# Attention with global rows and a two-layer MLP on one core: a transposition of gathered rows moved by one pair, three casts spread out, masks built earlier

## The chip, the cores and the metric

The kernel runs on one core of one Trainium2 chip. The metric is the device time of one execution in microseconds (us). A kernel is executed several times, and the times given are medians with the lowest and highest. All executions here counted as fast ones but one, the 368.65 us of e9_wst, which lies over 1.5% above that kernel's fastest; ratios leave it out. Each comparison was made on one chip, with the kernel before executed in the same rounds. A profile is one traced execution; its span is a little shorter than the time of that execution (368.7 us against 370.33 for the kernel before). Numbers of single instructions come from such profiles.

## The reference

```python
# q, k, v: (8, 8, 576, 64) float32; global_idx: 8 sorted positions
mask = np.abs(pos[:, None] - pos[None, :]) <= 32
mask = mask | is_global[:, None] | is_global[None, :]
scores = np.where(mask, 0.125 * q @ k^T, -1e9)
attn = softmax(scores) @ v                      # (8, 8, 576, 64)
x = attn.transpose(0, 2, 1, 3).reshape(4608, 512)
h = x @ w_in                                    # (512, 2048)
g = s * maximum(h, 0)**2 + b
return g @ w_out                                # (2048, 512) -> float32 (4608, 512)
```

The axes are batch, head, sequence and head dimension. Each query sees a band of 65 keys and the 8 global keys; the 8 global queries see everything.

## The kernel before

The kernel treats two heads at once. There are 32 such pairs, four to a batch. Pairs 0 to 4 make up the start, where little but attention can run. From pair 5 on, each pair has eight slots, and a quantum of MLP matmuls of earlier tokens fills each slot. TensorE always has work of the MLP as long as nothing in front of it in its own list waits. The profiles show what happens when something does: while VectorE stood 7.64 us at one copy, nothing behind that copy in VectorE's list ran.

The rows of the eight global positions need extra work. They are collected by an indirect DMA (`gather`) for eight pairs at once, rounded to bfloat16 by VectorE (`round_kq`), turned by TensorE (`turn`), and put among the keys and queries of each pair (`put_kq`).

```python
def gather(bb, ts="kq"):
    ...
    for t in ts:
        nc.gpsimd.indirect_dma_start(out=gfs[bb][:, i], in_=src[t]..., in_offset=...grow[bb]...)

def globals_of(bb):
    ...
    def round_kq():                                    # L384
        nc.vector.tensor_copy(out=gb[:, 0:2], in_=gfs[bb][:, 0:2])
    def turn():                                        # L391
        for i in range(2):
            for hh in range(2):
                nc.tensor.transpose(ps[r, i], gb[r, i], ident[r, r])
    ...
    return round_kq, turn

def put_kq(p):                                         # L431: K, L435: Q
    nc.vector.tensor_copy(out=view(ktile[p], ...), in_=view(gkt[bb]...))
    nc.vector.tensor_copy(out=view(qbufs[p % 3]...), in_=view(gqd[bb % 2]...))
```

K from pair 8 on comes in its natural order (`load_nat`), is rounded by ScalarE (L189) and transposed by a DMA (`turn_k`, L224). V arrives as float32 and is cast to bfloat16 (`cast_v`, L232). The masks are small VectorE products (`build_masks`). ScalarE makes the exponentials of the scores (`e`, L510), VectorE multiplies them by the mask (`em`, L513, "the em product"), and TensorE multiplies `em` by V (`po`, L532, "P·V").

The start, and the loads that follow it:

```python
first_pair(0, {
    1: [lambda: cast_v(A, 0), lambda: build_masks((2,))],
    3: [lambda: build_masks((3, 4))],
    4: [clear_q2, lambda: select(1)],
})
flush()
steps0[0]()
load_v(nc.gpsimd, 4)
load_kq(5)
for p in (1, 2, 3):
    cast_v(G, p)                  # G: GpSimd
for p in (1, 2, 3, 4):
    first_pair(p, ...)            # with put_v, load_v(5), load_w_out(0), load_kq(6)
flush()
warm(12)                          # dummy matmuls that keep TensorE busy, L741
scatter(0)                        # GpSimd puts the global rows of batch 0 into xt, L580
load_w_out(1)
load_v(nc.gpsimd, 6)
...
load_w_out(2); load_kq(7); load_v(nc.gpsimd, 7); load_w_out(3)
```

And the loop from pair 4 on, of which the change moves two lines:

```python
for p in range(4, NPAIR):
    ...
    if p == 5:
        nc.vector.memset(natk[0:1, 0, 0, 0, 0:8], 0.0)   # holds back the load of K(8)
    for j in {4: (), 5: (8, 9), 6: (10,), 7: (11, 12)}.get(p, (p + 5,)):
        load_nat(nc.sync, "k", j); load_q(j); load_nat(nc.sync, "v", j)
    if p % 8 == 4 and p + 4 < NPAIR:
        gather((p + 4) // 8)
    ...
    if p >= 6 and p + 2 < NPAIR:
        ...                                  # round_k and round_q of later pairs, ScalarE
        at(7, turn_k, p + 2)
        at(7, put_v, None, p + 2)
    if p % 8 > 4 and p + 3 < NPAIR:
        if p % 8 == 5:
            steps = globals_of((p + 4) // 8)
            at(7, steps[0])                  # round_kq
        elif p % 8 == 6:
            at(1, steps[1])                  # turn
    if 9 <= p < 17:
        adds.extend(wpiece(p - 9))           # 0.5 MB weight pieces for the bias
```

`at(s, f)` puts `f` into slot `s` of the pair.

The softmax here doesn't subtract the row's maximum and nothing guards it: scores larger than these inputs give would overflow.

Of the kernel before, what the change touches and what calls it, by code (L numbers as in the profile page):

```python
# [54 lines left out]
def view(ap, *dims):  # L55

    return bass.AP(
        tensor=ap.tensor, offset=ap.offset, ap=[list(ap.ap[0])] + [list(d) for d in dims]
    )
# [8 lines left out]
def kernel(  # L68
# [86 lines left out]
    def load_kq(p):  # L155
        bi, hp = divmod(p, 4)
        for t in "kq":
            nc.gpsimd.dma_start(
                out=six[t][:NP6, p % NR].rearrange("p h j d -> p h (j d)"),
                in_=src[t][bi, 2 * hp : 2 * hp + 2].rearrange("h (p j) d -> p h (j d)", j=NJ),  # L160
            )

    def load_nat(eng, t, p):
        bi, hp = divmod(p, 4)
        if t == "q":
            dst = natq[:].rearrange("p n h j d -> p n (h j d)")[:, :, 0 : NCH * 2 * D]
            dst = dst.rearrange("p n (c h d) -> p n c h d", c=NCH, h=2)
        else:
            dst = natv if t == "v" else natk
        r = NG if t == "v" else 0  # L170
        for hh in range(2):
            o = src[t][bi, 2 * hp + hh, 0, 0].offset

            runs = [(0, NCH, KC)]
            if p == NPAIR - 1 and hh == 1:
                runs = [(0, NCH - 1, KC), (NCH - 1, 1, S - KC * (NCH - 1))]
            for c, nch, n in runs:
                eng.dma_start(  # L178
                    out=dst[r : r + n, p % NV, c : c + nch, hh],
                    in_=bass.AP(  # L180
                        tensor=src[t].tensor, offset=o + c * KC * D,
                        ap=[[D, n], [KC * D, nch], [1, D]],
                    ),
                )
# [9 lines left out]
    def load_q(p):  # L194
        if p >= NSIXQ:
            load_nat(nc.sync, "q", p)
            return
        bi, hp = divmod(p, 4)
        nc.sync.dma_start(
            out=natq[:NP6, p % NV].rearrange("p h j d -> p h (j d)"),  # L200
            in_=q[bi, 2 * hp : 2 * hp + 2].rearrange("h (p j) d -> p h (j d)", j=NJ),
        )
# [25 lines left out]
    def load_v(eng, p):  # L228
        load_nat(eng, "v", p)

    def cast_v(eng, p):
        eng(out=vring[:, p % NV], in_=natv[:, p % NV])  # L232
# [68 lines left out]
    def gather(bb, ts="kq"):  # L301

        if bb not in gfs:
            gfs[bb] = globp.tile([P, 3, D], FP32, tag="gf", name="gf")
        for t in ts:
            i = "kqv".index(t)
            nc.gpsimd.indirect_dma_start(  # L307
                out=gfs[bb][:, i], out_offset=None,
                in_=src[t].rearrange("b h s d -> (b h s) d"),
                in_offset=IndirectOffsetOnAxis(ap=grow[bb][:], axis=0),  # L310
            )
# [37 lines left out]
    def build_masks(cs):  # L349
        for c in cs:  # L350
            m = const.tile([P, W[c]], BF16, name=f"mask{c}", tag=f"mask{c}")
            x0 = LO[c] - P * c + WIN
            nc.vector.scalar_tensor_tensor(
                out=m[:], in0=band[:, x0 : x0 + W[c]], scalar=notg[:, c : c + 1],
                in1=gadd[c // (NCH - 1)][:, x0 : x0 + W[c]], op0=OP.mult, op1=OP.add,
            )
            masks.append(view(m[:], [0, 2], [1, W[c]]))
# [13 lines left out]
    def flush():  # L371
        ops, later[:] = list(later), []
        for f in ops:
            f()
# [297 lines left out]
    A, V, G = nc.scalar.copy, nc.vector.tensor_copy, nc.gpsimd.tensor_copy  # L672
# [40 lines left out]
    def select(p):  # L713

        ps = ps_m.tile([P, 2, NG], FP32, tag="moe", name="psg")
        for i, t in enumerate("kq"):
            for j in range(NJ):
                for hh in range(2):
                    nc.tensor.matmul(
                        ps[D * hh : D * hh + D, i], six[t][:NP6, p, hh, j], sel6[:NP6, j],  # L720
                        start=(j == 0), stop=(j == NJ - 1), skip_group_check=True,
                    )

        def put():
            nc.vector.tensor_copy(
                out=view(ktile[p], [P, NCH], [1, NG]), in_=view(ps[:, 0], [0, NCH], [1, NG])
            )
            for hh in range(2):
                r = slice(D * hh, D * hh + D)
                nc.vector.tensor_copy(  # L730
                    out=view(qbufs[p][r, hh, HB:], [P, NCH], [1, NG]),
                    in_=view(ps[r, 1], [0, NCH], [1, NG]),
                )

        later.insert(0, put)
# [7 lines left out]
    def first_pair(p, extra={}):  # L743


        if p % 4 == 0:
            open_batch(p // 4)
        bank = idle_bank()
        for s in range(NCH):
            prev, later[:] = list(later), []  # L750
            now = []
            if s > 1 if p == 0 else p > 1 or s == 0:
                warm(1, bank)
            qk(p, s)
            i = s - {0: 2, 1: 1, 4: 3}.get(p, 0)
            if i in (0, 1):
                (trans_b, trans_a)[i](p + 1, now)
            if p and s in (1, {1: 4, 4: 2}.get(p, 3)):

                pv(p - 1, (int(s == 1),))  # L760
                if s == 1:
                    pending.extend(norm_steps(p - 1))
            if s == 3 and p < 4:
                step()
            for f in prev + now:
                f()
            for f in extra.get(s, ()):
                f()
            if s == 1:
                step()  # L770
                if p == 4:
                    step()
            if s == 4 and p == 4:
                cast_v(A, 4)
# [53 lines left out]
    def clear_q2():  # L828
# [1 line left out]
        clear(qbufs[2][D:P, 0], LQ)  # L830

    first_pair(0, {
        1: [lambda: cast_v(A, 0), lambda: build_masks((2,))],
        3: [lambda: build_masks((3, 4))],
        4: [clear_q2, lambda: select(1)],
    })
    flush()
    steps0[0]()
    load_v(nc.gpsimd, 4)
    load_kq(5)  # L840
    for p in (1, 2, 3):
        cast_v(G, p)
    for p in (1, 2, 3, 4):
        first_pair(p, {
            0: [steps0[1], steps0[2]],
# [58 lines left out]
    for p in range(4, NPAIR):  # L904
        bi, hp = divmod(p, 4)
        nq = [1] * 8
        if bi == 1:
            nq = [0, 1, 1, 1, 1, 1, 1, 1] if hp else [0, 0, 0, 0, 0, 0, 1, 2]
        elif hp == 0:
            quanta[0] += 32  # L910
        if p == 5:

            nc.vector.memset(natk[0:1, 0, 0, 0, 0:8], 0.0)
        for j in {4: (), 5: (8, 9), 6: (10,), 7: (11, 12)}.get(p, (p + 5,)):
            if j < NPAIR:
                load_nat(nc.sync, "k", j)
                load_q(j)
                load_nat(nc.sync, "v", j)
# [3 lines that stand above are left out]
            for i in range(NG):  # L922
                nc.gpsimd.dma_start(
                    out=gvall[i : i + 1].rearrange("o (b h d) -> o b h d", b=B - 2, h=H),
                    in_=v[2:, :, ds(greg_p[i], 1), :].rearrange("b h o d -> o b h d"),
                )
        ex = {}

        def at(s, f, *a):
            ex.setdefault(s, []).append(lambda: f(*a))  # L930

        if p >= 6 and p + 2 < NPAIR:

            todo = {6: (8,), 8: (11,), 9: (12,)}.get(
                p, {0: (p + 3, p + 4), 3: (p + 2, p + 3)}.get(hp, ())
            )
            for i, j in enumerate(todo):
                if j < NPAIR:
                    x = 4 if p in (8, 9) else 4 * i
                    at(1 + x, round_k, j)  # L940
                    at(3 + x, round_q, j)
            at(7, turn_k, p + 2)
            at(7, put_v, None, p + 2)
        if p % 8 > 4 and p + 3 < NPAIR:
            if p % 8 == 5:
                steps = globals_of((p + 4) // 8)
                at(7, steps[0])
            elif p % 8 == 6:
                at(1, steps[1])
        if 10 <= p < 18:  # L950
            for s in (4, 7):
                if adds:
                    at(s, adds.pop(0))
        if 9 <= p < 17:
            adds.extend(wpiece(p - 9))
        if p == 18:
            assert not adds
            at(2, bias)
        if p > 18 and hp in (0, 3) and held_rows:
            at(2, release)  # L960
            at(6, release)
        run_pair(p, nq, ex)
# [43 lines left out]
```

## Time and profile before

| | kernel before |
|---|---|
| time, median of 3 (lowest to highest) | 369.65 us (367.6 to 370.06) |
| span of the profile | 368.7 us |
| TensorE busy | 346.2 us, 94% |
| longest stand of TensorE | 7.33 us at 56.4 us, for the turning of gathered rows |
| second longest | 2.52 us at 21.6 us, for V of pair 0 |
| pair 5 starts / pair 6 starts / pair 7 starts | 45.69 / 54.88 / 73.69 us |

"Pair n starts" means in this document that the first score matmul of the pair starts. The difference of two starts is how long a pair took, so the starts say where a gain arises and whether it lasts. The prediction below shows the views themselves: TensorE's row of slices first, then its waits by what ended them, then the instructions around the two longest, with the start and duration of each and, in brackets, the idle time of its engine just before and what ended it. The number after an L is a source line.

How the loads' landings were read matters as well. The instruction that issues a DMA can end long before the data arrive (the second gather's ended at 53.01 us, its rows landed at 63.45); the arrival is in the completion records of the trace. The natural K of pair 8 landed at 51.2 and 55.0 us (two halves), the two gathers of the second group at 63.02 and 63.45 us, 12.3 and 11.4 us after their issues began; the quickest gather of this kernel took 2.4 us.

The trace also records the clock that TensorE was granted. In the kernel before it changes between 1.00 and 0.50 ("full" and "half" here), among other times, at 17.04, 30.69, 58.00 and 68.24 us, in the changed kernel at 25.6, 39.25 and 42.66 us. In each kernel these times are whole multiples of 3.41 us apart; a "window" of the clock is one such stretch of 3.41 us.

Three more lines of the timeline of the kernel before are needed for the comparison, the end of the head and the rounding of the natural K of pair 8 by ScalarE:

```profile
40.40 2.76 PE L741 MATMUL psw<-dummy 128*128 128x512 bf16 x11
43.10 2.75 PE L603 MATMUL psh<-xt,win_t 128*128 128x512 bf16 x12
...
57.43 0.73 ACT L189 CAST natb<-natk 120x640 bf16<-120x640 f32 x1
```

The dummy matmuls take 2.76 us at full clock (granted 1.00 from 40.40 to 43.10 us; twelve were issued, the trace holds records of eleven), the first MLP matmuls follow at 43.10 us, and ScalarE finds its K there: no line has a bracket, so none of them waited.

### The profile page before, as it was taken

The numbers are of one execution on the slowest core, as the hardware profiler recorded it, in microseconds if no ns is written. First come the engines' busy times: TensorE is split into PE (matmuls) and PEld (weight loads), VectorE is DVE, ScalarE is ACT, GpSimd is POOL, SyncE is SP. The second block draws the span as 40 slices with busy tenths as digits, with TensorE's granted clock in tenths as the row PEclk, the third lists the DMA queues.
The fourth block names the chain that finished last, engine by engine and source line by source line (L and its number), as shares of the span: only waits on it lengthen the run. The fifth ranks groups of instructions, "written<-read, shape, count | busy, mean of one in ns | idle before, by whom it ended". The sixth has DMA issues, their size and how long they took to land.

```text
span 368.7 us, 7769 instructions
## 1 busy us (share of the span) xinstructions
PE 346.2 (94%) x2758; PEld 184.9 (50%) x2793; DVE 240.3 (65%) x636; ACT 228.2 (62%) x439; POOL 85.6 (23%) x164
## 2 busy tenths in 40 slices
PE   6769992999999999999999999999999999999996
PEld 3435441455544554557755555555557644444444
DVE  6678671777777789767777687767776643432431
ACT  6758682665876678667766776677647742611610
POOL 6972573204021411141403100311030001000000
PEclk9958996799999999999999999999999999999999
DMA  5999799997978897885568975995232011002002
GB/s 119 193 191 206 118 208 218 177 191 157 201 158 170 160 196 171 186 182 110 116 147 205 222 148 142 211 220 110 88 129 75 2 48 68 0 30 85 1 31 85
DMA packets 121186, 50.48 MB, mean 137 GB/s; under 512 B 107298, under 2 KB 114114, under 8 KB 121146
## 3 DMA queue, kind: packets, MB, share of 16 engines
q1 hardware_dynamic: 112106, 37.50, 48.5%
q0 software_dynamic: 8544, 12.03, 16.2%
q8 instruction: 22, 0.36, 0.4%
q10 hardware_dynamic: 496, 0.43, 0.4%
q14 instruction: 18, 0.15, 0.1%
HBM read 42.20 MB, written 9.44 MB: 140 GB/s over the span
## 4 chain that ended last, share of the span: by engine, by line
PE 79%; DVE 5%; DMA 5%; POOL 4%; issue 4%; ACT 2%; POOLq 0%; ACTq 0%
PE psh L603 31%; PE pso L622 30%; PE po L532 8%; PE pss L506 6%; DMA gf<-in_q_dram,grow 3%; PE pst L447 2%; DVE qbd L494 1%; DVE em L513 1%; PE pst L460 1%; POOL gf L307 1%; DMA natk<-in_k_dram 1%; DMA sixq<-in_q_dram 1%; POOL natv L178 1%; POOL wout_t L361 1%; ACT e L510 1%
## 5 line engine op out<-in xcount | busy, mean ns | idle before, releaser
L603 PE MATMUL psh<-xt,win_t 128*128 128x512 bf16 (+4 forms) x691 | 139.7, 343 | 0.6
L622 PE MATMUL pso<-wout_t,g 128*128 128x512 bf16 (+1 forms) x575 | 135.1, 373 | 1.6 <-issue 1.1
L610 ACT ACTIVATE r<-psh 128x512 bf16<-128x512 f32 x144 | 88.5, 616 | 65.5 <-PE psh L603 62.2
L510 ACT ACTIVATE e<-pss 128x384 bf16<-128x384 f32 (+1 forms) x160 | 76.9, 484 | 48.9 <-PE pss L506 48.1
L603 PEld LDWEIGHTS <-win_t 128*128 128x128 bf16 x704 | 64.2, 98 | 55.3 <-issue 2.7
L613 DVE TENSOR_TENSOR g<-r 128x512 bf16<-128x512 bf16 x144 | 59.1, 423 | 43.9 <-ACT r L610 43.5
L622 PEld LDWEIGHTS <-g 128*128 128x128 bf16 x592 | 56.3, 98 | 59.1
L513 DVE TENSOR_TENSOR em<-e,mask 128x384 bf16<-128x384 bf16 (+1 forms) x160 | 62.2, 391 | 30.2 <-ACT e L510 30.2
L506 PE MATMUL pss<-qbd,kt 128*128 128x384 bf16 (+1 forms) x160 | 52.6, 332 | 2.8 <-DVE qbd L730 1.2
L580 POOL COPY xt<-xg 128x4 bf16 x64 | 19.2, 299 | 99.8 <-DVE xt L569 96.4
L642 DVE SCALAR_TENSOR_TENSOR osb<-pso,s_bc,bias_row 128x512 f32<-128x512 f32 (+1 forms) x25 | 18.2, 727 | 27.9 <-PE pso L622 27.9
L232 POOL CAST vring<-natv 128x640 bf16<-128x640 f32 x27 | 22.3, 844 | 54.9 <-PE po L532 51.8
L569 DVE TENSOR_TENSOR xt<-po,rep 128x600 bf16<-128x600 f32 x32 | 24.9, 780 | 2.4 <-ACT rep L566 1.1
L506 PEld LDWEIGHTS <-kt 128*128 128x128 bf16 x160 | 16.0, 100 | 20.2 <-DVE qbd L435 2.6
L563 ACT ACTIVATE ln<-po 128x640 f32<-128x640 f32 x32 | 22.5, 704 | 5.7 <-PE po L532 5.4
L566 ACT ACTIVATE rep<-ln 128x640 f32<-128x640 f32 x32 | 24.1, 752 | 0.1
L532 PE MATMUL po<-em,vring 128*64 128x160 bf16 (+3 forms) x448 | 20.3, 227 | 3.0 <-DVE vring L424 2.5
L532 PEld LDWEIGHTS <-vring 128*64 128x64 bf16 x448 | 16.0, 112 | 13.3 <-issue 8.7
L532 PE MATMUL po<-em,onesb 128*64 128x160 bf16 (+2 forms) x448 | 19.7, 226 | 0.2 <-DVE xt L569 0.2
L494 DVE COPY qbd<-pst 64x600 bf16<-64x600 bf16 x20 | 15.6, 778 | 4.6 <-ACT qbd L494 4.2
L489 DVE COPY qbd<-pst 64x600 bf16<-64x600 bf16 x38 | 17.8, 468 | 0.9
L189 ACT CAST natb<-natk 120x640 bf16<-120x640 f32 x24 | 17.8, 740 | 0.0
(106 smaller groups left out, 228.0 us busy)
## 6 DMA issues: line engine op xcount, KB each, us to landing
natv<-in_v_dram SPq DMA_DIRECT2D x55, 150.0 KB, 4.0
natk<-in_k_dram SPq DMA_DIRECT2D x47, 150.0 KB, 3.1
out_dram<-osb SPq DMA_DIRECT2D x23, 256.0 KB, 2.9
natq<-in_q_dram SPq DMA_DIRECT2D x37, 150.0 KB, 3.1
wst<-in_moe_w_out_dram POOLq DMA_DIRECT2D x8, 512.0 KB, 6.0
out_dram<-osbh SPq DMA_DIRECT2D x9, 256.0 KB
win_t<-in_moe_w_in_dram POOLq DMA_DIRECT2D x2, 1024.0 KB, 12.5
wout_t<-in_moe_w_out_dram POOLq DMA_DIRECT2D x4, 512.0 KB, 10.5
```

The lines of the kernel that those rows point to most:

```text
L232: eng(out=vring[:, p % NV], in_=natv[:, p % NV])
L506: nc.tensor.matmul(ps[:], ktile[p][:, P * c : P * c + P], qbufs[p % 3][:, :, LO[c] : HI[c]])
L510: nc.scalar.activation(e[:], ps[:], AF.Exp, scale=SCALE)
L513: later.append(lambda: nc.vector.tensor_mul(em[:], e[:], masks[c]))
L532: nc.tensor.matmul(po[D * hh : D * hh + D, a : a + n], onesb[:] if part else vring[:, p % NV, c, hh], emt[(p, c)][:, hh, x : x + n], start ...
L563: nc.scalar.activation(ln[:], po[:, LQ : 2 * LQ], AF.Ln)
L566: nc.scalar.activation(rep[:], ln[:], AF.Exp, scale=-1.0)
L569: lambda: nc.vector.tensor_tensor(out=view(xt[:, hp, x0:], [KC, NCH], [HB, 2], [1, HB]), in0=halves(po[:, 0:LQ]), in1=halves(rep[:]), op=O ...
L603: nc.tensor.matmul(psh[:, d0 : d0 + n], win_t[:, a, f * P : f * P + P], xt[:, a, x0 : x0 + n], start=(a == 0 and j == 0), stop=(a == 3), s ...
L610: nc.scalar.activation(r[:], psh[:], AF.Relu)
L613: later.append(lambda g=g, r=r: nc.vector.tensor_mul(g[:], r[:], r[:]))
L622: nc.tensor.matmul(pso[:, 0:nn], gl[f][:, u * P : u * P + P], wout_t[:, f, n0 : n0 + nn], start=(f == 0), stop=(f == 15),)
```

## The change

The intent has three parts. First, the rows that were gathered during pair 4 of a group of eight are rounded at the end of pair 6 instead of pair 5, and turned in pair 7 instead of pair 6, so that VectorE and TensorE don't wait for the gathers. Secondly, GpSimd's three V casts, which ran back to back, are put between its DMA issues, so that VectorE's em product, which took 2.77 us beside the three, need not take so long. Thirdly, masks 3 and 4 are built one stage sooner.

```diff
     first_pair(0, {
-        1: [lambda: cast_v(A, 0), lambda: build_masks((2,))],
-        3: [lambda: build_masks((3, 4))],
+        1: [lambda: cast_v(A, 0), lambda: build_masks((2, 3, 4))],
         4: [clear_q2, lambda: select(1)],
     })
     flush()
     steps0[0]()
+
+    cast_v(G, 1)
     load_v(nc.gpsimd, 4)
+    cast_v(G, 2)
     load_kq(5)
-    for p in (1, 2, 3):
-        cast_v(G, p)
+    cast_v(G, 3)
...
         if p % 8 > 4 and p + 3 < NPAIR:
-            if p % 8 == 5:
+            if p % 8 == 6:
                 steps = globals_of((p + 4) // 8)
                 at(7, steps[0])
-            elif p % 8 == 6:
+            elif p % 8 == 7:
                 at(1, steps[1])
```

## The prediction

> **What bounds the kernel now.** I began with the page: the slices of the span, then who waited for whom on TensorE, then the timeline around the two holes that these show, then the DMA issues and landings. From the page, slices of 9.2 us:
>
> ```profile
> PE   6769992999999999999999999999999999999996
> ...
> PEclk9958996799999999999999999999999999999999
> DMA  5999799997978897885568975995232011002002
> ```
>
> TensorE is full from the eighth slice to the last (346.2 of 368.7 us busy), so the time falls only if a hole in front closes. There are two places: slice 7 (55 to 64 us) where PE shows 2 tenths, with the clock low in slices 7 and 8, and the softer start up to 28 us. The DMA engines are at 7 to 9 tenths through most of the first half. TensorE's waits, by who ended them (in total, times, longest):
>
> ```profile
> PE psg L391 <- DVE gb L384: 7.5, 2, 7.3
> PE po L532 <- DVE vring L424: 2.5, 1, 2.5
> ...
> PE pss L506 <- DVE qbd L730: 1.2, 1, 1.2
> ```
>
> The first and second are what the change is aimed at. The first in the timeline (start, duration, engine, line; in brackets the idle time before and its end):
>
> ```profile
> 56.09 0.34 PE L506 MATMUL pss<-qbd,kt 128*128 128x384 bf16 x1
> ...
> 63.47 0.23 DVE L384 CAST gb<-gf 128x128 bf16<-128x128 f32 x1 [7.64 <-DMA gf<-in_q_dram,grow]
> ...
> 63.76 0.31 PE L391 MATMUL psg<-ident,gb 64*64 64x64 bf16 x4 [7.33 <-DVE gb L384]
> ...
> 64.00 1.89 PE L603 MATMUL psh<-xt,win_t 128*128 128x512 bf16 x4
> ```
>
> VectorE rounds the gathered K and Q rows of the second group of eight pairs at the end of pair 5; TensorE turns them early in pair 6. The gathers left GpSimd's queue at 50.69 and 52.03 us but the second landed at 63.45, because 0.5 MB weight pieces and K, Q, V loads were in flight (204 to 215 GB/s in those windows). VectorE, then TensorE, stand 7.3 us. Afterwards four psh matmuls take 1.89 us where 1.03 us is usual: the clock records say half rate from 58.00 to 68.24 us. The second hole:
>
> ```profile
> 20.89 2.77 DVE L513 TENSOR_TENSOR em<-e,mask 128x384 bf16<-128x384 bf16 x1
> ...
> 21.28 2.16 POOL L232 CAST vring<-natv 128x640 bf16<-128x640 f32 x3
> ...
> 23.58 0.47 DVE L424 COPY vring<-gvx 8x640 bf16<-8x640 bf16 x1
> ...
> 24.10 1.01 PE L532 MATMUL po<-em,vring 128*64 128x160 bf16 x14 [2.52 <-DVE vring L424]
> ```
>
> One em product takes 2.77 us instead of the 0.34 to 0.39 of its kind, exactly while three GpSimd casts run back to back; the V copy behind it, and the first P·V matmuls behind that, wait.
>
> [...]
>
> **The change part by part.** No instruction is added or removed in numbers: the order of TensorE, VectorE and GpSimd changes, ScalarE's and SyncE's do not.
>
> (1) *Rounding and turning one pair later.* Rounding now stands at the end of pair 6, turning in pair 7. Without the hole pair 6 takes what pair 5 took, 54.88 − 45.69 = 9.19 us, instead of 73.69 − 54.88 = 18.81. So 9.6 us come free: 7.3 of standing and about 2.3 from the half clock. Is the gather there by then? VectorE reached the rounding right after a copy that ended at 55.84; a pair later that is 65.0, and the data landed at 63.45. Yes, with 1.6 us to spare. The turned rows are first wanted by pair 8's K and Q, late in pair 7, some 5 us after the turning. For the batches turned near 140 and 213 us nothing waits now and nothing will.
>
> But not all 9.6 us stay. What pairs 8 and 9 need comes through SyncE's queue, which did not wait for TensorE in this stretch: from 45.65 to 81.51 us it issues almost without a pause[...] (one K half took 5.11 us to issue). Its landings I read from the trace's completion records. K of pair 8, transposed, landed at 72.6; VectorE would ask for it (81.24 before) at about 71.6: 1.0 us of waiting. K of pair 9:
>
> ```profile
> 78.91 2.60 SPq L224 DMA_TRANSPOSE kt<-natb  x1
> ...
> 90.08 0.16 DVE L431 COPY kt<-gkt 128x40 bf16<-128x40 bf16 x1
> ...
> 90.62 0.10 PEld L506 LDWEIGHTS <-kt 128*128 128x128 bf16 x1
> ```
>
> It is issued at 78.91 behind V of pair 12 and landed at 84.6; VectorE used it at 90.08. The slack was 5.5 us, so of 9.6 us only about **5.4** remain, the rest (1.0 + 3.2) becoming a new wait for transposed K at the ends of pairs 7 and 8. Later pairs have more: pair 10's K landed 9.9 us ahead, pair 11's 7.1, and there SyncE begins to wait for TensorE instead. [...] I take **1.2** off for that (two chances in three).
>
> (2) *Three casts one at a time.* Each cast is 0.72 us (2.16/3). The first moves to about 18.1, where VectorE is idle until 18.81; the two V descriptor writes (1.94 us) follow, then the second cast at about 20.8 to 21.5, then K and Q (1.55 us), then the third at about 23.0. Only the second meets the em product of 20.89, which then ends near 21.85 instead of 23.66, and P·V starts near 22.35 instead of 24.10: **1.75** us. [...] The later issue of the V and K loads costs nothing: they queue behind a weight piece landing at 32.62. [...] I take **1.5**. The DMA stretch of (1) starts when batch 0 is scattered (40.48), so it moves along with this.
>
> (3) *Masks sooner.* Two mask builds (0.70 us) leave the path at 14.44, ahead of the select copies that held TensorE 1.2 us (the third wait above), and go to about 11.5, where VectorE waits for 12.78 anyway. Pair 1 starts some 0.6 us sooner, but its turning of pair 2's Q waits for a load that landed at 17.34 and started at 17.39. **0**.
>
> Sum: 5.4 − 1.2 + 1.5 = 5.7 us.
>
> **The rivals.** *All 9.6 us stay* (with (2), −11 us, 358.5): for it, SyncE's order is unchanged and the loads run five pairs ahead; against it, the 1.40 DMA share at 73.7 to 81.8 us and the landing at 84.6. I give it one in ten. *The hole only moves*: the gather lands later than 65 us, or VectorE meets another load, and gain (1) falls to 2 to 3 us. For it, an earlier TensorE start also crowds the DMA; against it, issue order is the same and there were 1.6 us. *Casts make nothing*: VectorE is caught by each cast in turn, or the V copy waits for the copies from PSUM (to 21.55); then −4 us in all. [...]
>
> **Range and chances.** 369.65 − 5.7 = 363.95; the less likely large gain weighs a little more than the small one, so 363.7 us. The 8-in-10 range runs from 360.5 ([...]half the DMA wait avoided) to 367.0 (stand moved, casts worthless). Faster by over 2% needs under 362.3: 0.23. Same: 0.76. Slower: 0.01.
>
> **What would show it.** Right: the 7.3 us wait on the turning is gone, em at 21 us lasts under 1.2 us, P·V starts near 22.3; slices 7 and 8 have full clock; VectorE or TensorE wait some 3 us for transposed K near 80 us; from pair 10 on both kernels run alike, at a constant distance. Wrong: no wait for transposed K (then the gain is near 10), a new long wait at the rounding itself, a half clock lasting several windows after 80 us, or a distance that shrinks after pair 12, which would mean that DMA bounds those pairs too.

## The result

| | before | after |
|---|---|---|
| time, median of 4 (lowest to highest) | 369.86 us (367.6 to 370.69) | 363.88 us (363.36 to 364.2) |
| ratio after / before, 95% interval | | 0.9847 [0.9801, 0.9892] |
| span of the profile | 368.7 us | 362.5 us |
| TensorE busy | 346.2 us (94%) | 343.7 us (95%) |

A ratio is the mean time of one kernel's fast runs over the mean of the other's fast runs of the same rounds, so it is not quite the ratio of the medians. The change saves 1.5%, which is within 2%: the class is "same", although the interval excludes 1. The predicted time of 363.7 us was 0.2 us off, and the class was right. As shown further down, the way there was partly another than predicted.

The same rows of the page of the changed kernel, slices of 9.1 us:

```profile
PE   6798897899999999999999999999999999999996
...
PEclk9659899999999999999999999999999999999999
DMA  5999999999999799786449984983341011002002
```

The seventh slice, which showed 2 tenths, now shows 7, and the clock is at 9 tenths or more from the sixth slice on. The DMA row stands at 9 tenths without a break from the second to the thirteenth slice: TensorE's work moved forward, and the loads did not get lighter. TensorE's waits in the changed kernel, in total, times, longest:

```profile
PE pst L460 <- DMA sixq<-in_q_dram: 2.2, 2, 1.7
PE pss L506 <- ACT e L510: 1.7, 2, 1.4
PE pss L506 <- DVE qbd L435: 1.5, 3, 0.9
...
PE psg L391 <- DVE gb L384: 0.6, 1, 0.6
...
PE po L532 <- DVE vring L424: 0.5, 1, 0.5
```

The two waits at which the change aimed fell from 7.5 to 0.6 and from 2.5 to 0.5 us. Three waits moved up in their place, 2.2, 1.7 and 1.5 us in total where the kernel before has 0.5, 0.4 and 0.7, and the first of them is for a load. The timeline of pairs 6 and 7:

```profile
58.37 1.03 PE L603 MATMUL psh<-xt,win_t 128*128 128x512 bf16 x4
59.19 0.72 ACT L189 CAST natb<-natk 120x640 bf16<-120x640 f32 x1 [1.58 <-DMA natk<-in_k_dram]
...
60.84 0.30 PE L506 MATMUL pss<-qbd,kt 128*128 128x320 bf16 x1 [1.44 <-ACT e L510]
...
67.04 0.31 PE L506 MATMUL pss<-qbd,kt 128*128 128x320 bf16 x1 [0.89 <-DVE qbd L435]
...
68.51 0.25 PE L391 MATMUL psg<-ident,gb 64*64 64x64 bf16 x4
```

Groups of psh matmuls take 1.03 us now, not 1.89, and the clock is full (granted 1.00 from 54.59 to 68.24 us). The turning at 68.51 waits for nothing. But ScalarE stands 1.58 us for the natural K of pair 8, the exponentials behind that rounding in its list come late, and TensorE then stands 1.44 us for one of them. The head of the kernel:

```profile
20.57 0.80 POOL L232 CAST vring<-natv 128x640 bf16<-128x640 f32 x1
20.83 0.58 DVE L431 COPY kt<-gkt 128x40 bf16<-128x40 bf16 x1
...
21.41 0.34 DVE L513 TENSOR_TENSOR em<-e,mask 128x384 bf16<-128x384 bf16 x1
...
22.20 1.01 PE L532 MATMUL po<-em,vring 128*64 128x160 bf16 x14 [0.47 <-DVE vring L424]
...
37.73 0.45 PE L460 MATMUL pst<-ident,sixq 96*64 96x96 bf16 x12 [1.67 <-DMA sixq<-in_q_dram]
...
39.52 3.88 PE L741 MATMUL psw<-dummy 128*128 128x512 bf16 x10 [0.18 <-issue]
...
43.24 2.75 PE L603 MATMUL psh<-xt,win_t 128*128 128x512 bf16 x12
```

The em product takes 0.34 us instead of 2.77, and P·V starts at 22.20 us, 1.90 sooner than before. The rest of the head loses this again. TensorE stands 1.67 us for Q of pair 5, which landed at 37.69 us against 36.4 before. TensorE was busy for 1.74 us of the window from 35.84 to 39.25 us, and the next window, to 42.66 us, was at half clock (granted 0.50): the twelve dummy matmuls (ten records) took 3.88 us; before, they (eleven records) took 2.76 us. So the first MLP matmul starts at 43.24 us where it started at 43.10 before. In the kernel before, a window with 1.66 us busy (54.59 to 58.00 us) was likewise followed by half clock; windows with 1.92 us busy (after, 59.73 to 63.14 us) and 1.75 (e7, 37.88 to 41.30) were followed by full clock. What decides it is not shown. In the chain of work that ended last (start, duration, what) this head is carried by two loads:

```profile
21.91 15.78 DMA sixq<-in_q_dram
...
46.20 12.88 DMA natk<-in_k_dram
```

The first is that Q, the second is half of the natural K of pair 8: 12.88 us, where the median from issue to landing of such a half over this run is 3.3 us. Most of the time from 22 to 59 us on that chain is now waiting for loads: 28.66 of 37 us.

The starts of pairs in the profiled executions, for the two kernels and for the experiments that follow:

| pair | before | after | again | e1 | e4 | e5 | e6 | e7 | e8 | e10 |
|---|---|---|---|---|---|---|---|---|---|---|
| 2 | 25.45 | 23.55 | 23.37 | 25.29 | 23.02 | 23.80 | 22.90 | 23.89 | 24.07 | 25.89 |
| 4 | 35.58 | 32.31 | 34.92 | 34.63 | 32.64 | 33.10 | 32.44 | 33.34 | 33.32 | 35.73 |
| 5 | 45.69 | 45.83 | 45.01 | 44.73 | 43.70 | 43.21 | 45.79 | 43.45 | 43.52 | 45.84 |
| 6 | 54.88 | 54.94 | 54.17 | 54.78 | 53.00 | 52.33 | 54.91 | 52.62 | 52.63 | 54.95 |
| 7 | 73.69 | 67.04 | 66.53 | 65.90 | 70.53 | 64.81 | 65.86 | 65.00 | 63.50 | 67.65 |
| 8 | 81.84 | 75.47 | 74.96 | 74.33 | 78.67 | 73.24 | 74.29 | 73.44 | 72.16 | 75.79 |
| 9 | 90.84 | 84.47 | 84.69 | 84.06 | 87.67 | 82.24 | 83.29 | 83.18 | 82.53 | 86.16 |
| 10 | 100.24 | 93.88 | 94.52 | 93.74 | 97.08 | 91.95 | 93.34 | 93.72 | 93.14 | 96.56 |
| 12 | 119.23 | 112.88 | 113.51 | 113.28 | 116.63 | 110.94 | 112.34 | 112.71 | 112.66 | 116.09 |
| 31 | 293.16 | 287.01 | 287.64 | 287.48 | 290.60 | 285.07 | 286.47 | 286.84 | 286.79 | 290.01 |

Read the columns before and after. At pair 4 the change is 3.27 us ahead; at pair 5 it is 0.14 behind; pair 6 takes 12.10 us instead of 18.81, which is the whole gain of 6.7; and the distance is 6.36 at pair 10 and still 6.15 at pair 31. The column "again" is a second execution of the same changed kernel: at pair 4 it is only 0.66 us ahead of the kernel before, at pair 5 0.68. So a difference at the start is not to be read from one execution.

### The profile page after: what moved, and what is told of

Its sections match the earlier page's. It is cut to its first block, busy times and chain, and to the rows that moved or that the text cites. A ratio compares the mean times of both kernels' runs of the same rounds, so it can differ in the third digit from the quotient of the medians.

```text
span 362.5 us, 7769 instructions
## 1 busy us (share of the span) xinstructions
PE 343.7 (95%) x2758; PEld 183.3 (51%) x2793; DVE 239.2 (66%) x636; ACT 227.5 (63%) x439; POOL 85.0 (23%) x164
## 4 chain that ended last, share of the span: by engine, by line
PE 76%; DMA 9%; DVE 6%; POOL 3%; issue 3%; ACT 2%; SPq 0%; ACTq 0%; POOLq 0%; DVEq 0%
PE pso L622 31%; PE psh L603 29%; PE po L532 7%; PE pss L506 5%; DMA natk<-in_k_dram 5%; DMA sixq<-in_q_dram 4%; DVE qbd L494 2%; PE pst L447 2%; PE psw L741 1%; POOL gf L307 1%; DVE em L513 1%; DVE xt L569 1%; POOL sixk L158 1%; ACT r L610 1%; ACT rep L566 1%
## 5 line engine op out<-in xcount | busy, mean ns | idle before, releaser
L603 PE MATMUL psh<-xt,win_t 128*128 128x512 bf16 (+4 forms) x691 | 137.9, 340 | 0.7
L513 DVE TENSOR_TENSOR em<-e,mask 128x384 bf16<-128x384 bf16 (+1 forms) x160 | 60.6, 381 | 26.5 <-ACT e L510 26.2
L232 POOL CAST vring<-natv 128x640 bf16<-128x640 f32 x27 | 22.2, 829 | 55.4 <-PE po L532 46.5
L506 PEld LDWEIGHTS <-kt 128*128 128x128 bf16 x160 | 15.7, 99 | 20.9 <-DVE qbd L435 3.5
```

Source lines behind the costliest of these rows:

```text
L506: nc.tensor.matmul(ps[:], ktile[p][:, P * c : P * c + P], qbufs[p % 3][:, :, LO[c] : HI[c]])
L513: later.append(lambda: nc.vector.tensor_mul(em[:], e[:], masks[c]))
L603: nc.tensor.matmul(psh[:, d0 : d0 + n], win_t[:, a, f * P : f * P + P], xt[:, a, x0 : x0 + n], start=(a == 0 and j == 0), stop=(a == 3), s ...
```

## The experiments

The first theory was that the prediction's account holds: the parts add up, and some of the gain in pair 6 comes back as waits that loads set. The rivals were that the parts overlap (the head alone already lets the gathers land sooner, so each alone would give most of the gain), and that the gain given back is not set by loads but by other work of pair 6. The unchanged repeat of the changed kernel measures how far executions differ. Numbers of an experiment with one profile come from one execution. The two executions of the changed kernel differ by 2.61 us at pair 4, 0.82 at pair 5 and 0.63 at pair 31; where two kernels differ by no more than that, the timed ratio decides.

**e1_turn: the later turning alone**, on the kernel before.

```diff
-            if p % 8 == 5:
+            if p % 8 == 6:
                 steps = globals_of((p + 4) // 8)
                 at(7, steps[0])
-            elif p % 8 == 6:
+            elif p % 8 == 7:
                 at(1, steps[1])
```

> The turning moved a pair later, casts and masks as before. Overlap theory (late turning and earlier casts attack the same 7.3 us hole in pair 6, so their gains do not add): pair 5 starts as before at 45.7 us and the gathers land near 63.4 us, the hole is gone, and the waits that I predicted appear: VectorE waits 3 to 4 us for transposed K of pairs 8 and 9 (landing near 84.6 us); total 4 to 5.5 us less than before, about 364.4 to 365.9. Additive rival (the casts gave nothing by pair 5, so turning alone is the whole change): 5.7 to 6.3 us less, with ScalarE waiting for natural K of pair 8 in pair 6 as in the changed kernel.

Measured: 365.81 us (364.65 to 367.24), ratio 0.9908 [0.9845, 0.9971]. The hole is gone. ScalarE does not wait for natural K here, and yet pair 6 takes 11.12 us (65.90 − 54.78), not 9.19. Here the K of pair 9 becomes tight, as the prediction expected, if hardly more than that: it landed at 82.8 us, VectorE took it in the same moment, in 0.60 us instead of 0.16, and TensorE waited 0.57 us behind it.

```profile
82.79 0.60 DVE L431 COPY kt<-gkt 128x40 bf16<-128x40 bf16 x1
...
84.06 0.31 PE L506 MATMUL pss<-qbd,kt 128*128 128x320 bf16 x1 [0.57 <-DVE qbd L435]
```

**e2_casts: the spread casts alone.**

```diff
     steps0[0]()
+    cast_v(G, 1)
     load_v(nc.gpsimd, 4)
+    cast_v(G, 2)
     load_kq(5)
-    for p in (1, 2, 3):
-        cast_v(G, p)
+    cast_v(G, 3)
```

> The three casts apart, turning and masks as before. Overlap theory: GpSimd's queue runs about 3 us ahead (batch 0 is scattered near 37.5 instead of 40.5 us), the gathers land near 58 to 60 instead of 63.45 us, so the hole in pair 6 shrinks from 7.3 us to 2 to 4 us and its half clock largely goes: 4 to 6 us less than before although pair 5 starts no sooner. Additive rival: the gain of the start is eaten before pair 5 (as in the changed kernel, -0.1 us there), the hole stays over 6 us, 0 to 1 us less than before.

Measured: 367.42 us (365.63 to 369.81), ratio 0.9922 [0.9863, 0.9982]. P·V of pair 0 starts at 22.38 us instead of 24.10. In the profile the hole stays whole; the gathers landed at 62.3 us, 1.1 sooner than before. This profile is of the slowest of the four executions (369.81 us; the others took 365.63 to 367.73), so how long the hole was in the faster ones is not known. The saving, 2.9 us by the ratio (0.7 to 5.1), lies between the two expectations, and its interval reaches into both.

```profile
PE psg L391 <- DVE gb L384: 7.5, 1, 7.5
```

**e3_masks: the masks alone.**

```diff
-        1: [lambda: cast_v(A, 0), lambda: build_masks((2,))],
-        3: [lambda: build_masks((3, 4))],
+        1: [lambda: cast_v(A, 0), lambda: build_masks((2, 3, 4))],
```

> Masks sooner alone. Both theories: pair 1 starts 0.6 us sooner and waits that much longer for the load of pair 2's Q (landing near 17.4 us), so nothing: within 0.5 us of before, and the hole of 7 us in pair 6 is still there. Rival of its own: 0.6 us or more stays and moves GpSimd's queue, then 1 to 2 us less.

Measured: 370.53 us (369.64 to 371.06), ratio 1.0022 [0.9965, 1.0079]. The masks alone save nothing that these runs can show (about ±2 us), as predicted.

**e4_head: casts and masks together, without the later turning** (the two edits above).

> Casts and masks together, turning as before: the change less its first part. Overlap theory: as the casts alone, 4 to 6 us less than before with a hole of 2 to 4 us in pair 6, so that the later turning is worth only 0 to 2 us on top. Additive rival: 0 to 1 us less than before, the hole as large as before.

Measured: 368.35 us (367.8 to 369.49), ratio 0.9974 [0.9918, 1.003]. Pair 5 starts 2.0 us sooner, the gathers landed at 59.75 us, and the hole is still 5.6 us long. If the parts overlapped, this kernel would have most of the gain, 4 to 6 us; it has a quarter of a per cent, at most 3.0 us by its interval. The turning alone gives 0.92% (3.4 us of 370), the head alone 0.26% (1.0 us), their sum is 4.4 us, and the whole change gave 5.7 and, repeated, 4.9 us. With e2's 2.9 us for the head the sum would be 6.3. The intervals are wide enough for that to be one sum. **The overlap theory fell in the size that was stated**; an overlap of a us or two is not excluded.

**a2_again: the changed kernel, unchanged.**

> The changed kernel once more, on the chip of the next three runs: 363.4 to 364.5 us, with ScalarE waiting 1 to 2 us for natural K of pair 8 in pair 6. [...]

Measured: 364.72 us (363.87 to 364.81), ratio 0.9868 [0.9829, 0.9908]. In this execution ScalarE's wait for natural K is 0.9 us, pair 6 takes 12.36 us, and pair 5 starts at 45.01. So single waits vary by about 1 us from execution to execution, and the timed median (0.2 us above the expected range) by less. And here the transposed K of pairs 9 and 10 is met: it landed at 83.47 and 94.18 us, and VectorE took it in the same moment:

```profile
83.50 0.51 DVE L431 COPY kt<-gkt 128x40 bf16<-128x40 bf16 x1 [0.23 <-DMA kt<-natb]
...
94.20 0.17 DVE L431 COPY kt<-gkt 128x40 bf16<-128x40 bf16 x1 [0.75 <-DMA kt<-natb]
```

TensorE stood 0.56 us behind each of the two, and pairs 8 and 9 together took 19.56 us (94.52 − 74.96), against 18.40 before and 18.41 in the first execution of the change.

The next four start from the changed kernel and take away one suspected wait each.

**e5_kq5: K and Q of pair 5 asked for ahead of V of pair 4.**

```diff
     cast_v(G, 1)
-    load_v(nc.gpsimd, 4)
-    cast_v(G, 2)
     load_kq(5)
+    cast_v(G, 2)
+    load_v(nc.gpsimd, 4)
     cast_v(G, 3)
```

> The changed kernel with K and Q of pair 5 asked for ahead of V of pair 4, against the wait of 1.67 us for Q of pair 5 in pair 4. Theory (the start's 3.3 us of gain at pair 4 were lost to this load and to the half clock and dummies after it): Q lands near 35.5, the wait goes, pair 5 starts 1 to 2.5 us sooner, and the total is 0.5 to 2 us less than the changed kernel. Rival (the saturated loads fix pair 9 at about 84 us whatever comes before): pair 5 sooner, pairs 6 to 8 longer by the same, total within 0.4 us.

Measured: 364.23 us (362.24 to 365.26), ratio 0.9872 [0.9832, 0.9913]. Q of pair 5 landed at 34.89 us instead of 37.69 and nobody waited for it, the dummies took 2.76 us at full clock, and pair 5 started at 43.21, which is 2.6 us sooner than in the changed kernel. In the profiled execution, the fastest of the four, 1.9 us of this remain at the end (a span of 360.6 us), but the timed ratio does not show it: 0.9872 stands beside 0.9847 and 0.9868 of the changed kernel.

**e6_nomemset: the memset that holds back the load of natural K of pair 8 removed.**

```diff
-        if p == 5:
-
-            nc.vector.memset(natk[0:1, 0, 0, 0, 0:8], 0.0)
```

> The changed kernel without the small memset that holds back SyncE's loads of pair 8 until pair 5 starts (45.8 us); they may then start near 39 to 40 us. Theory (pair 6 is held by ScalarE's wait of 1.6 us for natural K of pair 8): it lands before 57 us, the wait goes, pair 6 takes 10 to 11 us instead of 12.1, and the total is 1 to 2 us less than the changed kernel. Rival (the DMA engines are full from 43 to 70 us, so another load takes the place): gathers, weights or Q of pair 5 or 6 land later and the total is within 0.5 us or more.

Measured: 363.10 us (362.47 to 364.13), ratio 0.9831 [0.9787, 0.9875]. The K landed at 47.4 us instead of 59.1, and ScalarE's wait is gone:

```profile
57.46 0.73 ACT L189 CAST natb<-natk 120x640 bf16<-120x640 f32 x1
```

Pair 6 took 10.95 us instead of 12.10, so the wait was worth 1.2 us there. The gathers landed at 62.22 us, still ahead of their use (in the unaltered repeat they landed at 62.97, so this is not the edit's doing for certain). A new wait of 1.0 us for the transposed K of pair 10 came up behind, and at pair 10 only 0.5 us of the 1.2 are left. The ratio is the lowest so far and still within the interval of the unaltered change.

**e7_warm4: 4 dummy matmuls instead of 12 ahead of the first MLP quantum.**

```diff
-    warm(12)
+    warm(4)
```

> The changed kernel with 4 instead of 12 dummy matmuls ahead of the first MoE matmuls; in the changed kernel these 12 took 3.88 us at half clock and ended 3.8 us after the scatter of batch 0. Theory (they stand on the path since the start became faster): pair 5 starts 1.5 to 2.5 us sooner and 0.5 to 2 us remain at the end. Rival [...]: pair 5 starts within 1 us of 45.8 and the total is 0 to 1.5 us more.

Measured: 364.07 us (363.91 to 366.67), ratio 0.9881 [0.9829, 0.9934]. At full clock (the four dummies took 1.04 us) fewer dummies free nothing, since the MLP's first matmul then waits for GpSimd's scatter:

```profile
40.86 2.75 PE L603 MATMUL psh<-xt,win_t 128*128 128x512 bf16 x12 [1.67 <-POOL xt L580]
```

Pair 5 started at 43.45 us, about as in e5 with all twelve. So the 2.4 us by which it leads the changed kernel come from an execution in which Q of pair 5 was not late and the clock stayed full, and not from the dummies. What happened to the lead is the useful part: it was 2.0 us at pair 8, 1.3 at pair 9 and 0.2 at pair 10, where VectorE waited for the transposed K:

```profile
93.40 0.18 DVE L431 COPY kt<-gkt 128x40 bf16<-128x40 bf16 x1 [1.44 <-DMA kt<-natb]
```

In the changed kernel the same copy stands at 93.46 us without a wait. Arriving sooner did not let it run sooner.

**e8_three: e5, e6 and e7 together**, in five rounds.

```diff
     cast_v(G, 1)
-    load_v(nc.gpsimd, 4)
-    cast_v(G, 2)
     load_kq(5)
+    cast_v(G, 2)
+    load_v(nc.gpsimd, 4)
     cast_v(G, 3)
...
-    warm(12)
+    warm(4)
...
-        if p == 5:
-
-            nc.vector.memset(natk[0:1, 0, 0, 0, 0:8], 0.0)
```

> The changed kernel with all three: K and Q of pair 5 first, no memset ahead of SyncE's loads, 4 dummies. Theory (the start and the wait in pair 6 are then free, and the next bound is transposed K of pairs 9 and 10, whose loads meet the bias weights that GpSimd asks for near 81 us): pair 5 starts near 43.3 us, pair 9 near 81.5 to 82.5, VectorE waits 1 to 3 us for transposed K of pair 10, and the total is 361 to 363 us. Rival (the pieces add up freely): 359.5 to 361.

Measured: 363.92 us (363.47 to 365.38), ratio 0.9833 [0.9807, 0.986], in five rounds. At pair 7 this kernel is 3.5 us ahead of the changed one, at pair 9 1.9, at pair 10 0.7 and at pair 12 0.2. VectorE stands for the transposed K of pairs 9 and 10:

```profile
82.09 0.35 DVE L431 COPY kt<-gkt 128x40 bf16<-128x40 bf16 x1 [1.62 <-DMA kt<-natb]
...
92.82 0.18 DVE L431 COPY kt<-gkt 128x40 bf16<-128x40 bf16 x1 [1.52 <-DMA kt<-natb]
```

So in e7 and e8 nearly all that is won ahead of pair 9 is returned by pair 10, in e6 half of it, and what returns it is a load: VectorE stands for it by name. The profiled execution of e5 is the exception; it kept 1.9 us to the end, with pair 10 at 91.95 us. The moment at which the loads let pair 10 start therefore differs by some 2 us between kernels and executions, and no addition to the change moved the timed ratio for certain.

One comparison on record points to what these loads met. In the four profiles with the old turning (before, e2, e3, e4) the transposing DMA of the K of pair 10 went out before the first 0.5 MB weight piece for the bias, landed 2.6 to 3.8 us after its issue, and VectorE used the K 8.7 to 9.9 us later. In all profiles with the turning moved, and in e10, the first piece went out within a microsecond of it or sooner, it took 5.7 to 11.2 us, and in all of these but the first profile of the change (2.6 us of room) VectorE took the K within 0.03 us of its landing. The kernels differ in more than this, so it is a strong hint and not a test.

**e9_wst: e8 with the 0.5 MB weight pieces for the bias one pair later**, to see whether it is they that delay the K of pair 10.

```diff
-        if 10 <= p < 18:
+        if 11 <= p < 19:
...
-        if 9 <= p < 17:
-            adds.extend(wpiece(p - 9))
-        if p == 18:
+        if 10 <= p < 18:
+            adds.extend(wpiece(p - 10))
+        if p == 19:
...
-        if p > 18 and hp in (0, 3) and held_rows:
+        if p > 19 and hp in (0, 3) and held_rows:
```

> The same with the bias weight pieces (8 of 0.5 MB) asked for a pair later. Theory: transposed K of pair 10 lands 2 to 4 us sooner, the wait for it is under 0.5 us, and the total is 1 to 2 us less than the run before it, 359.5 to 361.5. Rival (the DMA engines are full on average, so another transfer waits): within 0.5 us of the run before it.

Measured: 364.02 us (361.02 to 368.65), ratio 0.9805 [0.977, 0.9841], with the widest spread of all. Of these runs one was slow (368.65); the fast ones spread from 361.02 to 365.98, and the verdict is "unclear". The K of pair 10 landed at 94.2 us, later than in e8, and VectorE waited 3.0 us for it. The edit missed its aim: GpSimd issued the first two pieces at 81.44 and 84.09 us, only 1.1 and 2.4 later than in e8 and still ahead of that K's transposition (86.27). So it does not test the theory.

Pair 6 is worth a look here: as in e6 the memset is gone and natural K landed early (46.0 us), but ScalarE stood 2.2 us for a V (L232) instead, and the pair took 12.12 us again; in e11 3.0 us and 12.66.

**e11_wst2: e8 with the pieces two at a time and from pair 11 on.**

```diff
-        if 10 <= p < 18:
-            for s in (4, 7):
+        if 12 <= p < 19:
+            for s in (1, 2, 3, 4):
...
-        if 9 <= p < 17:
-            adds.extend(wpiece(p - 9))
-        if p == 18:
+        if p in (11, 13, 15, 17):
+            for i in range(2):
+                adds.extend(wpiece(p - 11 + i))
+        if p == 19:
...
-        if p > 18 and hp in (0, 3) and held_rows:
+        if p > 19 and hp in (0, 3) and held_rows:
```

> The run with all three (kq5, no memset, 4 dummies), and the eight bias weight pieces asked for two at a time from pair 11 on, so that none is in flight while the loads for pairs 9 and 10 are. Theory (pair 10 is fixed by these pieces, 233 GB/s at 81.8 to 90.8 us, pushing transposed K of pair 10 to 92.8 us): it lands before 90 us, pair 10 starts at 91 to 92.5 instead of 93.1 us, and the total is 361 to 362.5 us, the fastest of all. Rival (a stand moved is only taken up by the next load): pair 10 or 11 starts as before and the total is within 0.7 us of 363.9.

Measured: 365.03 us (363.92 to 368.66), ratio 0.9844 [0.9827, 0.9861]. The experiment missed its aim. Nothing on GpSimd's list held the pieces back, so it issued the first two at 83.67 us, long before TensorE was in pair 11, and the K of pair 10 landed at 94.7 us (the profile is of the slowest execution of this kernel):

```profile
83.67 1.48 POOL L886 DMA_DIRECT2D wst<-in_moe_w_out_dram  x2
...
94.73 0.17 DVE L431 COPY kt<-gkt 128x40 bf16<-128x40 bf16 x1 [4.01 <-DMA kt<-natb]
```

Two pieces at once went with the longest wait for this K in any run. That is in line with the pieces delaying it, but the change without any piece in flight at that time was not run. Whether pair 10 would then start sooner is open.

**e10_early: the rival cure, on the kernel before.** The rounding and turning stay where they were, and the gathers go out ahead of a 0.5 MB weight piece and V of pair 6, right after the scatter.

```diff
     warm(12)
+    for i in (1, 2, 3):
+        rows_of(i)
     scatter(0)
+    gather(1)
     load_w_out(1)
     load_v(nc.gpsimd, 6)
-    for i in (1, 2, 3):
-        rows_of(i)
...
-        if p % 8 == 4 and p + 4 < NPAIR:
+        if p % 8 == 4 and 4 < p and p + 4 < NPAIR:
             gather((p + 4) // 8)
```

> The kernel before, turning where it was, with the gather of the second group issued ahead of the three weight pieces instead of behind them. If the hole in pair 6 is nothing but the late landing of the gather, it lands near 48 us, the hole is gone without any later turning, and the time falls like that of the later turning alone: 3 to 6 us less than before, 364.5 to 367; pair 6 takes about 11 us rather than 9.2, from ScalarE's rounding of pair 8. Rival (the turning's place in the order matters by itself, or the weights that then come later take its place): under 2 us less.

Measured: 367.84 us (366.69 to 369.29), ratio 0.9937 [0.9908, 0.9965], so 2.3 us of gain where 3 to 6 were expected. The gathers landed at 48.45 us, 15 sooner, and the hole is still not closed. V of pair 6, put behind them, landed at 56.0 us instead of 50.5, and ScalarE meets a V that is not there:

```profile
56.18 0.72 ACT L232 CAST vring<-natv 128x640 bf16<-128x640 f32 x1 [3.96 <-DMA natv<-in_v_dram]
...
58.91 0.25 PE L391 MATMUL psg<-ident,gb 64*64 64x64 bf16 x4 [2.42 <-DVE gb L384]
```

The wait of TensorE still has the name of the rounding of gathered rows, although these rows had long landed: VectorE was kept from them by ScalarE, and ScalarE by V. Here hurrying one transfer delayed another. The later turning leaves the order of transfers in every queue as it was.

No version was shown to beat the changed kernel: e6 and e8 have ratios of 0.9831 and 0.9833, within the interval of the change and next to its 0.9847; e9's 0.9805 comes with a spread of 5.0 us among its fast runs.

## Why the prediction was right or wrong

**Right: the cause and its removal.** The 7.3 us stand and the half clock after it (58.00 to 68.24 us, granted 0.50) are gone, in the change and in every run with the later turning; e2 and e3, which lack it, keep stands of 7.5 and 7.2 us, and e4 one of 5.6. The gathers were there in time, as said, with more room than the 1.6 us (the second landed at 58.19 us and its rounding came at 67.96; in the repeat at 62.97 and 67.45).

**Right: the direct effect of the casts.** The em product went from 2.77 to 0.34 us and P·V started 1.90 us sooner; 1.75 was said. It is the same in all fourteen profiles: P·V starts at 24.05 to 24.55 us in the four with the casts together and at 22.00 to 22.73 in the ten with the casts apart. Which VectorE instruction takes longer beside the casts is not fixed: in e1 and e10 it was a copy of K, of 1.96 and 2.44 us, and in e3 three instructions had 0.52, 0.76 and 0.91 us, one with each cast. In the change it was a copy of 0.58 us (0.16 to 0.20 elsewhere) that met the second cast, and not the product.

**Right, as far as ±0.6% can show: masks 0** (e3: 1.0022, interval across 1). **Right in these profiles: a constant distance from pair 10 on** (6.36 us there, 6.15 at pair 31; in the repeat 5.72 and 5.52).

**Wrong: the step "without the hole pair 6 takes what pair 5 took, 9.19 us".** It took 12.10. Of the 9.6 us that this step set free, 6.7 came. e6 and e1 take the remainder apart. With no wait for a load in pair 6 it took 10.95 and 11.12 us, so about 1.8 us belong to the pair itself. On TensorE nearly all of it is standing and not work: in e6 TensorE is idle for 1.79 us of pair 6 and 0.10 of pair 5, and 1.45 of this is a wait for VectorE's copy of the Q of pair 7 (L435), the last thing before pair 7 starts. The same wait is 1.61 us in e1 and 0.89 in the changed kernel. What makes VectorE late is not shown. In pair 6 ScalarE rounds the K and Q of pair 8, 0.73 and 0.84 us, which pair 5 does not; before, this fell into the hole and cost nothing. That the roundings make up these 1.8 us is my reading of their durations, no run took them out of the pair. The other 1.2 us are the wait for natural K of pair 8 (e6 took it away), which the prediction did not see: it looked only at transposed K.

**Wrong in size: the step "the rest (1.0 + 3.2) becoming a new wait for transposed K at the ends of pairs 7 and 8".** For the K of pair 8 VectorE waited in no run. For the K of pair 9 it did not wait in the profiled execution:

```profile
83.70 0.16 DVE L431 COPY kt<-gkt 128x40 bf16<-128x40 bf16 x1
```

That K had landed at 81.7, not at 84.6, because the DMA stream did not stay in place: its transposition was issued at 75.98 us, 2.9 sooner than before. The completion records give a likely reason, GpSimd's queue being done with the gathers 5 us sooner. But the wait is real: in the repeat of the changed kernel the K of pairs 9 and 10 cost 1.2 us, e1 lost 1.0 us in the same two pairs, and in e6, e7 and e8 it shows as waits of 1.0 to 1.6 us, which return some or all of what these had won. So the mechanism held at 0 to 1.2 us where 4.2 were predicted. One more reading failed, "later pairs have more": the K of pair 10, with 9.9 us of room before, had 2.6 us in the changed kernel and none in the repeat. In all, the prediction was right that loads take back some of the 9.6 us and that this ends by pair 10, but in the profiled execution what was taken, 2.9 us in pair 6 and 0.3 in pair 7 (8.43 us instead of 8.15), was taken one to two pairs earlier and not by transposed K. Its own sign for that case, a gain near 10 us when no wait for transposed K appears, came out otherwise for this reason: pair 6 had kept the difference.

**Wrong: the 1.2 us for a new stretch at half clock after 80 us.** The figure was the author's estimate. No such stretch came: from 42.66 us on the clock is full (granted 1.00). Where VectorE did stand 3.0 and 4.0 us for the K of pair 10, in e9 and e11, a window at half clock followed (95.02 to 98.43 and 94.86 to 98.28 us; in e11 the granted clock was 0.83 on average from 93 to 103 us). That the step failed because its stand of 3.2 us did not occur is my reading.

**Wrong in size: the step "I take 1.5" for the casts.** The 0.25 us taken off the worked-out 1.75 were the author's estimate. In the profiled execution nothing of it reached pair 5 (+0.14 us), because TensorE stood 1.67 us for Q of pair 5 and the dummies then ran at half clock (3.88 us instead of 2.76). In the repeat 0.68 us reached pair 5, in e2 1.18, in e4 1.99; in e5 and e7, without that wait and at full clock, 2.48 and 2.24. Timed, the head alone gave 1.0 us with an interval from a loss of 1.1 to a gain of 3.0. The statement that the later issue of K and Q "costs nothing" looks wrong in the profiles of before and after (Q of pair 5 landed 1.3 us later), but not in the rest: issued at 20.6 to 20.9 us, as before, it landed at 36.40 to 37.48 (before, e1, e3, e10), and issued at 21.8 to 22.3 at 36.69 to 38.16 (six profiles), with no order in it. What the step left out is that this Q lands near 37 us either way, so that a start that comes to it sooner can be stopped there (in the change, e4 and e6, by 1.0 to 1.7 us).

The sum: predicted −5.4 + 1.2 − 1.5 = −5.7 us. Profiled: −6.7 in pair 6, +0.3 in pair 7 and +0.1 ahead of them, and after pair 7 hardly anything; −6.2 at the end of the span. Two errors, too much given back to transposed K and too much credited to the head, had opposite signs. That the time was right to 0.2 us is in part luck.

What stays open: why natural K of pair 8 landed late enough to be waited for in the change and not in e1, what makes VectorE late at the end of pair 6, whether the weight pieces set the start of pair 10, and whether any of e5 to e9 is really a few tenths of a per cent faster than the change.

## What to carry to other kernels

When an engine stands for a transfer among many others, try moving the use later and not only asking sooner: here the later use gave 3.4 us by itself (1.1 to 5.7), and the earlier gather 2.3 (1.3 to 3.4), which passed the wait on to V. The intervals overlap, so that one is worth more is not shown; that the hole closes with the one and keeps 2.4 us with the other is. Before counting a closed hole as gain, list what other engines do inside it for free, and every load that the stages after it need, raw and transformed, with its landing time; the gain shrinks at each load that would be asked for before it lands. And follow the starts of stages through both traces: a lead that melts between two stages points to the wait that eats it, even when the end time shows nothing.
